# A relu behind a copy, the first queries in two transfers, and form jobs spread anew, in a three-layer kernel on one core

## The chip, the core and the metric

The kernel runs on one core of a Trainium2 chip. The metric is the device time of one execution in microseconds (us), as the median of several runs. The core has a matrix engine (TensorE, here PE, with its weight loads shown apart as PEld), a vector engine (VectorE, DVE), an activation engine (ScalarE, ACT), GpSimd (POOL) and SyncE (SP). Each works through a queue of its own in order, and semaphores tie the queues together. Transfers are issued on the queues of SP, ACT and POOL and carried out by 16 DMA engines. PE accumulates in PSUM banks; DVE and ACT read these and write to on-chip memory (SBUF). The clock that TensorE is granted has two levels here, 1.2 and 2.4 GHz, shown as 0.50 and 1.00.

## The reference

Three layers follow one another, for 4 batches of 448 positions and 768 channels (12 heads of 64):

```python
scores = q @ k.T / sqrt(64) - log(448)        # 48 heads, 448 x 448
x = sigmoid(scores) @ v                       # back to (4, 448, 768)

h = x.T @ U @ V                               # rank 32, along the positions
u = x + h.T
x = u + relu(u @ w_ch1) @ w_ch2               # 768 -> 3072 -> 768

gate = sigmoid(causal convolution of x, 5 taps a channel)
out = (gate * (x @ w_val)) @ w_out            # 768 -> 768 -> 768
```

q, k and v are float32, the weights come as float64. The products are made from a rounded part and a remainder of each factor: high by high, high by low and low by high, three matmuls in place of one (`mm3`, lines 439 to 441).

## The kernel before

**Attention** (to about 155 us) runs over 24 pairs of heads. A pair has one tile `kq`: keys of both heads on 128 partitions in `kq[:, 0]`, queries in `kq[:, 1]`. `load_kq` (L450) issues its transfers, `load_v` (L465) those of the values: 2 and 3 per pair. `kq` has three buffers. For the first two pairs the queries come in one transfer from an access pattern whose outermost step is the head (2 heads, 64 rows, 448 columns); keys and queries of the first pair go out on SP and ACT, of the second on ACT and SP. Later pairs use two SP transfers of 64 rows.

`prep_pair` (L484) makes the rounded parts `ks[:, 0]` (casts) and the remainders `ks[:, 1]` (subtractions on DVE, `low`). For the first pair the keys are cast by DVE (L494), the queries by ACT (L505). `scores` (L519) makes three 128 by 448 score tiles a pair, each from three products for each of two heads; ACT turns each into a sigmoid (L514), from one of three PSUM score tiles (`ps_s`). `scores_rest` and `attend` follow. Before the first scores PE runs `IDLE` matmuls on zeros (L1045). SP's order at the start is: first pair's keys, second pair's queries, six transfers of values, the third pair's load, constants (L654 to L662), then the fourth pair's load.

**The middle layer** (to about 834 us) has two halves, for batches 0, 1 and 2, 3, of six stages each. A stage has two chains and four `ch2` products. A chain (`seven`, L799) forms a 2 by 2 block product with seven products instead of eight. Their order is A11, A12, S2, S1, S3, S4, A22, each nine matmuls, into three PSUM banks x, y, z: A11 goes to x and is copied to p1; A12 goes to y; S2 adds to x, which is copied to u2 (L810); S1 goes to z, copied to p5; S3 adds to x, S4 adds to z, A22 adds to x. `both` (L866) adds two of them on DVE (L867) and puts off a `relu`, an ACT instruction (L861) and a DVE one (L862) that make the two parts of a hidden tile. The first of these, p1 plus y, is the chain's first sum, and its relu the chain's first relu.

Order is made while the program is written out. Steps that would wait are put in a list `deferred`, and each `flush()` writes out what is in it; `later` puts a step off by one flush more. A flush stands before each product, in some jobs, and in `weight` for as long as a weight form is not yet written.

Weights become forms by jobs (`pair_jobs`, `second_jobs`, `form_jobs`), one list for the whole layer, made by `plan`. `step()`, called after each product, takes one job off, now and then two, if the forms then held stay within `WS` = 10 tiles. `form_jobs` makes the seven or eight forms of each value and output weight block, 63 jobs in all, and stores them to memory. They are dealt out among the six stages of the second half: `share` = 13 to each until none is left, so 13, 13, 13, 13, 11, 0. In the same stages lie the gate's jobs, and at the ends of the first three the sums (`u_sums`, DVE at L600) for the value product.

**The last layer** (`val_chain`, `fin_chain`) uses `seven` too, with other `both` functions that put off no relu.

Of the kernel before, what the change touches and what calls it, by code (L numbers as in the profile page):

```python
# [12 lines left out]
AF = mybir.ActivationFunctionType  # L13
# [3 lines left out]
P = 128  # L17
B, H, S, D = 4, 12, 448, 64
# [6 lines left out]
NQ = NF // QUAD  # L25
TAPS = 5
PAD = TAPS - 1
SC = 112
# [10 lines left out]
NKC = 3  # L39
FILL = P - SC  # L40
USED = NKC * FILL
IDLE = 8
EARLY = 3
LATE = 5
PARTS = ("A11", "A12", "S2", "S1", "S3", "S4", "A22")
# [3 lines left out]
def tile_kernel(  # L49
# [18 lines left out]
    nc = tc.nc  # L68
    mm = nc.tensor.matmul
    f32 = lambda ap: ap.bitcast(F32)  # L70
    deferred = []

    def later(part):
        deferred.append(lambda: deferred.append(part))
# [99 lines left out]
    def done_with():  # L174
        live[0] -= len(spent)
        spent.clear()
# [236 lines left out]
    def ready_jobs(p):  # L413

        def job(n, half):
            def run():
                t = wtile(f"w2_{p}_{n}_{half}")
                nc.sync.dma_start(f32(t), stash["w2", n, half][:, :, :])
                forms[p, n, half] = t
            return 1, run, None  # L420

        return [job(n, half) for half in range(2) for n in range(QUAD)]
# [27 lines left out]
    def load_kq(p):  # L450

        kq = pools["kq"].tile([P, 2, S], F32, tag="kq", name=f"kq{p}")
        if p < 2:
            heads = bass.AP(
                tensor=kq_in.tensor, offset=kq_in[p, 0, 1].offset, ap=[[S, 2], [3 * S, D], [1, S]]
            )
            one, other = (nc.sync, nc.scalar) if p == 0 else (nc.scalar, nc.sync)
            one.dma_start(kq[:, 0], kq_in[p, :, 0])
            other.dma_start(kq[:, 1], heads)
        else:  # L460
            nc.sync.dma_start(kq[:D], kq_in[p, :D, :2])
            nc.sync.dma_start(kq[D:], kq_in[p, D:, 0::2])
        return kq
# [20 lines left out]
    def prep_pair(p):  # L484
        if p >= NP:
            return
        kq, vr = raws[p]
        ks = pools["ks"].tile([P, 2, 2, NSC, P], F32R, tag="ks", name=f"ks{p}")
        pairs[p] = ks, vr, {}
        rows = kq[:, :, :].rearrange("p t (c s) -> p t c s", c=NSC)  # L490
        fill = kq[:, 0, NKC * SC:NKC * SC + USED].rearrange("p (i s) -> p i s", i=NKC)

        def cast(op, r):
            op(ks[:, 0, r, :, :SC], rows[:, r])  # L494

        def low(r):
            nc.vector.tensor_sub(ks[:, 1, r, :, :SC], rows[:, r], f32(ks[:, 0, r, :, :SC]))  # L497

        if p == 0:
            cast(nc.vector.tensor_copy, 0)  # L500
        else:
            cast(nc.vector.tensor_copy, slice(0, 2))
        nc.vector.tensor_copy(ks[:, 0, 0, :NKC, SC:], fill)
        if p == 0:
            cast(lambda out, x: nc.scalar.activation(out, x, AF.Copy), 1)  # L505
            low(1)
            low(0)
        else:
            low(slice(0, 2))
        nc.vector.tensor_sub(ks[:, 1, 0, :NKC, SC:], fill, f32(ks[:, 0, 0, :NKC, SC:]))  # L510
# [288 lines left out]
    def seven(tag, weight_of, ts, both, last_of, step, before=None):  # L799

        def part(ps, ws, name, start=False):
            done_with()
            flush()
            w = weight_of(ws)
            for k in range(KH):
                mm3(ps, w, k, us[(ts, name), k], start and k == 0, k == KH - 1, skip_group_check=True)

        def copy(name, ps):
            t = pools["t"].tile([P, S], F32, tag="t", name=f"{name}_{tag}")[:, :]
            nc.scalar.activation(t, ps, AF.Copy)  # L810
            return t

        x = trio(f"x_{tag}")[:, 0, :S]
        z = bank(f"z_{tag}")[:, :S]
        part(x, "A11", "B11", True)
        p1 = copy("p1", x)
        step()
        if before:
            before()
        y = bank(f"y_{tag}")[:, :S]  # L820
        part(y, "A12", "B21", True)
        deferred.append(lambda: both(0, 0, p1, y))
        step()
        part(x, "S2", "T2")
        u2 = copy("u2", x)
        step()
        part(z, "S1", "T1", True)
        p5 = copy("p5", z)
        step()
        part(x, "S3", "T3")  # L830
        both(1, 1, p5, x)
        step()
        part(z, "S4", "B22")
        deferred.append(lambda: both(0, 1, u2, z))
        step()

        def last():
            part(x, "A22", "T4")
            last_of(x)
            step()  # L840

        return last

    def chain(p, c, step, before=None):

        b = halves[p]

        def weight_of(ws):
            w = weight(p, c, ws)
            if (p, c, ws) not in early:  # L850
                spent.append(1)
            return w

        def new(i, j):
            t = operand(f"h{c + i}_{b[j]}")
            hs[p, c + i, b[j]] = t
            return t

        def relu(i, j, x):
            t = new(i, j)  # L860
            nc.scalar.activation(t[:, 0], x, AF.Relu)  # L861
            deferred.append(lambda: nc.vector.scalar_tensor_tensor(  # L862
                t[:, 1], x, 0.0, f32(t[:, 0]), op0=ALU.max, op1=ALU.subtract
            ))

        def both(i, j, x, other):  # L866
            nc.vector.tensor_add(x, x, other)  # L867
            later(lambda: relu(i, j, x))

        return seven(f"{p}_{c}", weight_of, p, both, lambda x: relu(1, 0, x), step, before)  # L870

    def val_chain(k, gate, step, before=None):

        b = halves[0]
        z = lambda i, j: (x_of(b[j], k + KH * i), gate[k + KH * i][:, j])

        def both(i, j, x, other):
            nc.vector.tensor_add(x, x, other)
            out, g = z(i, j)
            deferred.append(lambda: nc.vector.tensor_mul(out, x, g))  # L880

        def last_of(x):
            out, g = z(1, 0)
            nc.vector.tensor_mul(out, x, g)

        return seven(f"val_{k}", lambda ws: fetched["val", k, ws, 0], "y", both, last_of, step, before)

    def fin_chain(p, k, src, step, before=None, end=False):

        b = halves[p]  # L890
        o = [pools["late"].tile([P, 2, S], F32, tag="late", name=f"o{p}_{k + KH * i}") for i in range(2)]
        have = set()

        def send(i, j):
            m = k + KH * i
            have.add((i, j))
            if end:
                nc.sync.dma_start(out[m, :, b[j]], o[i][:, j])
            elif (i, 1 - j) in have:
                nc.sync.dma_start(out[m, :, b[0]:b[-1] + 1], o[i])  # L900

        def both(i, j, x, other):
            nc.vector.tensor_add(o[i][:, j], x, other)
            send(i, j)

        def last_of(x):
            if not end:
                nc.scalar.activation(o[1][:, 0], x, AF.Copy)
                send(1, 0)
                return  # L910
            left, right = slice(0, S // 2), slice(S // 2, S)
            nc.scalar.activation(o[1][:, 0, left], x[:, left], AF.Copy)
            nc.vector.tensor_copy(o[1][:, 0, right], x[:, right])
            nc.scalar.dma_start(out[k + KH, :, b[0], left], o[1][:, 0, left])
            nc.sync.dma_start(out[k + KH, :, b[0], right], o[1][:, 0, right])

        return seven(
            f"fin{p}_{k}", lambda ws: fetched["out", k, ws, src], f"z{p}", both, last_of, step, before
        )

# [110 lines left out]
    def attention_phase():  # L1031
# [11 lines left out]
        idle = pools["ps_s"].tile([P, 2, 512], F32, tag="sc", name="idle")  # L1043
        for _ in range(IDLE):
            mm(idle[:, 0, :S], zeros[:, 0, :P], zeros[:, 0], start=True, stop=True)  # L1045
# [80 lines left out]
    def plan():  # L1126
# [9 lines left out]
        rest = []  # L1136
        for q in range(NQ):
# [17 lines left out]
            rest = w1[2:]  # L1155
# [3 lines left out]
            loads.remove(key)  # L1159
            loads.insert(len(ahead) - EARLY + 2 * i, key)  # L1160
        more = [job for kind in ("val", "out") for k in range(KH) for job in form_jobs(kind, k)]
        share = -(-len(more) // (NQ - 1))
        for q in range(NQ):
            give(pair_jobs(1, QUAD * q))
            a = pair_jobs(1, QUAD * q + 2) + (second_jobs(1, q) if q else ready_jobs(1))
            rest = more[:share]
            for i, job in enumerate(gate_jobs(halves[0], q)):
                rest.insert((2 * i + 1) * len(more[:share]) // 6 + i, (*job, None))
            for i, job in enumerate(a):
                give([job] + (rest[i // 2:i // 2 + 1] if i % 2 else []))  # L1170
            give(rest[len(a) // 2:])
            del more[:share]
# [288 lines left out]
```

## Time and profile before

| | |
|---|---|
| median of 3 runs | 1002.25 us (1001.76 to 1003.13) |
| profiled execution, whole | 1001.45 us |
| its span, first to last instruction | 999.7 us |
| PE busy | 983.3 us (98%) |
| PE weight loads | 837.9 us (84%) |
| DVE busy | 734.2 us (73%) |
| ACT busy | 463.7 us (46%) |
| mean granted TensorE clock | 0.996 |

All times within the execution count from the span's start. An engine's busy share is a mean over stages with different limits, so a shorter execution can only come from a stage where PE stands still or runs at the lower clock, or from work that PE itself no longer does. Matmuls follow each other before the one ahead has ended: a row of one matmul shows some 0.36 us, and one starts every 0.2 us.

### The profile page before, as it was taken

The numbers are of one execution on the slowest core, as the hardware profiler recorded it, in microseconds if no ns is written. First come the engines' busy times: TensorE is split into PE (matmuls) and PEld (weight loads), VectorE is DVE, ScalarE is ACT, GpSimd is POOL, SyncE is SP. The second block draws the span as 40 slices with busy tenths as digits, with TensorE's granted clock in tenths as the row PEclk, the third lists the DMA queues.
The fourth block names the chain that finished last, engine by engine and source line by source line (L and its number), as shares of the span: only waits on it lengthen the run. The fifth ranks groups of instructions, "written<-read, shape, count | busy, mean of one in ns | idle before, by whom it ended". The sixth has DMA issues, their size and how long they took to land.

```text
span 999.7 us, 14554 instructions
## 1 busy us (share of the span) xinstructions
PE 983.3 (98%) x5207; PEld 837.9 (84%) x5207; DVE 734.2 (73%) x1324; ACT 463.7 (46%) x871; POOL 22.6 (2%) x41
## 2 busy tenths in 40 slices
PE   6999999999999999999999999999999999999998
PEld 4455447988888999999999998998999999999997
DVE  2768798557668787879657988798878857993621
ACT  4657686345255363627243544536353532432321
POOL 0111200000000000000000000000000000000000
PEclk8999999999999999999999999999999999999999
DMA  5977856535447575766747555455644386834844
GB/s 139 262 201 206 216 154 172 169 87 140 138 122 220 182 220 176 219 194 206 272 145 260 186 204 195 156 201 203 220 139 176 103 311 213 277 111 128 260 152 171
DMA packets 82908, 187.51 MB, mean 188 GB/s; under 512 B 14948, under 2 KB 34644, under 8 KB 82836
## 3 DMA queue, kind: packets, MB, share of 16 engines
q1 hardware_dynamic: 78578, 171.07, 54.6%
q0 software_dynamic: 2976, 12.19, 4.1%
q10 hardware_dynamic: 1282, 3.33, 0.9%
q8 instruction: 41, 0.67, 0.3%
q14 instruction: 31, 0.25, 0.1%
HBM read 129.14 MB, written 57.41 MB: 187 GB/s over the span
## 4 chain that ended last, share of the span: by engine, by line
PE 80%; DVE 5%; ACT 1%; issue 1%; DVEq 0%; ACTq 0%
PE ch L439 12%; PE ch L440 11%; PE ch L441 11%; PE x L439 6%; PE x L441 6%; PE x L440 6%; PE z L439 3%; PE z L440 3%; PE z L441 3%; PE x_fin L439 1%; PE x_fin L441 1%; PE val L439 1%; PE val L440 1%; PE x_fin L440 1%; PE val L441 1%; PE y L441 1%
## 5 line engine op out<-in xcount | busy, mean ns | idle before, releaser
L439 PE MATMUL ch<-h,w 128*128 128x448 f32 x576 | 211.3, 367 | 0.0
L440 PE MATMUL ch<-h,w 128*128 128x448 f32 x576 | 210.5, 365 | 0.0
L441 PE MATMUL ch<-h,w 128*128 128x448 f32 x576 | 210.5, 365 | 0.0
L942 DVE TENSOR_TENSOR xs<-ch,xs 128x1344 f32<-128x1344 f32 x48 | 74.7, 1555 | 62.2 <-PE ch L441 62.1
L439 PEld LDWEIGHTS ch<-h,w 128*128 128x128 f32 x576 | 108.2, 188 | 10.5 <-issue 1.2
L441 PEld LDWEIGHTS ch<-h,w 128*128 128x128 f32 x576 | 108.2, 188 | 8.7
L440 PEld LDWEIGHTS ch<-h,w 128*128 128x128 f32 x576 | 108.2, 188 | 8.6
L514 ACT ACTIVATE a<-sc,bias 128x896 f32<-128x896 f32 x72 | 67.5, 1008 | 6.1 <-PE sc L526 5.6
L105 DVE SCALAR_TENSOR_TENSOR x_w<-x_w,r_w 128x384 uint32<-128x384 uint32 x84 | 47.0, 559 | 25.8 <-ACT x_w L101 19.4
L526 PEld LDWEIGHTS sc<-ks 64*128 64x128 f32 x432 | 38.8, 190 | 28.3 <-ACT ks L505 7.1
L526 PE MATMUL sc<-ks 64*128 64x448 f32 x432 | 53.8, 387 | 7.1 <-ACT ks L505 6.5
L557 PE MATMUL av<-a,vr 128*64 128x448 f32 x288 | 59.4, 548 | 0.1
L439 PE MATMUL x<-T,S 128*128 128x448 f32 x144 | 52.9, 367 | 2.3 <-ACT u L810 2.3
L101 ACT ACTIVATE x_w<-raw_w 128x384 f32<-128x384 f32 x84 | 45.4, 546 | 17.1 <-DMA k_h<-x_w 11.0
L441 PE MATMUL x<-T,S 128*128 128x448 f32 x144 | 52.8, 366 | 0.0
L440 PE MATMUL x<-T,S 128*128 128x448 f32 x144 | 52.6, 365 | 0.0
L557 PEld LDWEIGHTS av<-a,vr 128*64 128x64 f32 x288 | 18.5, 136 | 30.2 <-issue 26.7
L201 ACT ACTIVATE S<-raw_x_w 128x384 fp32r<-128x384 f32 x48 | 23.3, 518 | 41.7 <-DVE raw_x_w L253 21.9
L201 ACT ACTIVATE A<-x_w 128x384 fp32r<-128x384 f32 x36 | 18.3, 520 | 48.5 <-PE ch L441 43.2
L861 ACT ACTIVATE h<-p 128x448 fp32r<-128x448 f32 x48 | 27.5, 572 | 19.7 <-DVE p L867 19.7
L497 DVE TENSOR_TENSOR ks<-kq,ks 128x896 fp32r<-128x896 f32 (+1 forms) x25 | 26.3, 1055 | 7.4 <-ACT ks L505 7.4
L439 PEld LDWEIGHTS x<-T,S 128*128 128x128 f32 x144 | 27.0, 188 | 5.3 <-ACT u L810 3.0
(303 smaller groups left out, 2154.7 us busy)
## 6 DMA issues: line engine op xcount, KB each, us to landing
raw_w<-in_w SPq DMA_DIRECT2D x78, 384.0 KB, 3.7
kq<-in_kq SPq DMA_DIRECT2D x46, 224.0 KB, 4.5
raw_x_w<-k_w SPq DMA_DIRECT2D x24, 384.0 KB, 3.5
k_w<-x_w SPq DMA_DIRECT2D x42, 192.0 KB, 3.8
f_val_A<-s_val_A SPq DMA_DIRECT2D x21, 384.0 KB, 3.8
f_out_S<-s_out_S SPq DMA_DIRECT2D x20, 384.0 KB, 3.7
raw_w<-in_w POOLq DMA_DIRECT2D x18, 384.0 KB, 5.2
k_h<-x_w SPq DMA_DIRECT2D x36, 192.0 KB, 3.6
```

The source lines that it names most:

```text
L101: nc.scalar.activation(f32(x), f32(high), AF.Prelu, scale=2.0 ** -112, alpha=-(2.0 ** 32))
L105: nc.vector.scalar_tensor_tensor(x, x, 3, r, op0=ALU.logical_shift_left, op1=ALU.bitwise_or)
L201: nc.scalar.activation(t[:, 0], x, AF.Copy)
L439: mm(ps, wk[:, 0], x[:, 0], start=start, stop=False, **kw)
L440: mm(ps, wk[:, 0], x[:, 1], start=False, stop=False, **kw)
L441: mm(ps, wk[:, 1], x[:, 0], start=False, stop=stop, **kw)
L497: nc.vector.tensor_sub(ks[:, 1, r, :, :SC], rows[:, r], f32(ks[:, 0, r, :, :SC]))
L514: nc.scalar.activation(a[:, :, :], ps[:, :, :S], AF.Sigmoid, bias=bias, scale=1.0 / math.sqrt(D))
L526: mm(ps[:, h, :S].rearrange("p (c s) -> p c s", c=NSC), ks[r, tk, 0, c], ks[r, tq, 1, :, :SC], start=t == 0, stop=t == 2,)
L557: mm(att["ps"][D * h:D * h + D, :S], vr[:, h, c], a[:, h], start=c == 0, stop=False,)
L861: nc.scalar.activation(t[:, 0], x, AF.Relu)
L942: nc.vector.tensor_add(y, three[:, :, :S], y)
```

## The change

Four edits. The first pair's queries come in two transfers, one for each head, on ACT and on SP behind the keys; the second pair's load takes the form of the later ones, all on SP. The cast of these queries is split, half the partitions on ACT and half on DVE, and there are 10 idle matmuls in place of 8. In a chain the first sum is still written out at the same flush, but its relu is put into the list only once the copy of the third product has been written, and so stands behind this copy on ACT. The value and output form jobs are dealt 10, 10, 11, 14, 14 and the last 4 to the six stages, and the places of the gate's jobs among them follow the new share.

```diff
-IDLE = 8
+IDLE = 10
@@ load_kq
-        if p < 2:
-            heads = bass.AP(
-                tensor=kq_in.tensor, offset=kq_in[p, 0, 1].offset, ap=[[S, 2], [3 * S, D], [1, S]]
-            )
-            one, other = (nc.sync, nc.scalar) if p == 0 else (nc.scalar, nc.sync)
-            one.dma_start(kq[:, 0], kq_in[p, :, 0])
-            other.dma_start(kq[:, 1], heads)
+        if p == 0:
+            nc.sync.dma_start(kq[:, 0], kq_in[p, :, 0])
+            for h, queue in enumerate((nc.scalar, nc.sync)):
+                r = slice(D * h, D * h + D)
+                queue.dma_start(kq[r, 1], kq_in[p, r, 1 + h])
         else:
             nc.sync.dma_start(kq[:D], kq_in[p, :D, :2])
             nc.sync.dma_start(kq[D:], kq_in[p, D:, 0::2])
@@ prep_pair
-        def cast(op, r):
-            op(ks[:, 0, r, :, :SC], rows[:, r])
+        def cast(op, r, h=slice(0, P)):
+            op(ks[h, 0, r, :, :SC], rows[h, r])
...
         if p == 0:
-            cast(lambda out, x: nc.scalar.activation(out, x, AF.Copy), 1)
+            cast(lambda out, x: nc.scalar.activation(out, x, AF.Copy), 1, slice(0, D))
+            cast(nc.vector.tensor_copy, 1, slice(D, P))
             low(1)
             low(0)
@@ seven
         y = bank(f"y_{tag}")[:, :S]
         part(y, "A12", "B21", True)
-        deferred.append(lambda: both(0, 0, p1, y))
+        held = []
+        deferred.append(lambda: held.append(both(0, 0, p1, y, True)))
         step()
         part(x, "S2", "T2")
         u2 = copy("u2", x)
+        deferred.append(lambda: held[0] and held[0]())
         step()
@@ chain
-        def both(i, j, x, other):
+        def both(i, j, x, other, hold=False):
             nc.vector.tensor_add(x, x, other)
+            if hold:
+                return lambda: relu(i, j, x)
             later(lambda: relu(i, j, x))
@@ plan
-        share = -(-len(more) // (NQ - 1))
         for q in range(NQ):
...
+            share = (10, 10, 11, 14, 14, 10)[q]
             rest = more[:share]
             for i, job in enumerate(gate_jobs(halves[0], q)):
-                rest.insert((2 * i + 1) * len(more[:share]) // 6 + i, (*job, None))
+                rest.insert((2 * i + 1) * share // 6 + i, (*job, None))
```

## Rows read from the trace of the kernel before

**Rows 1.** Busy time by stretch: stretch, length, then PE, PEld, DVE, ACT, POOL busy, clock, DMA, GB/s.

```profile
950.00:1000.00 50.00, 45.98 (x223) 41.43 (x221) 10.98 (x19) 10.78 (x22) 0.00 (x0) 0.98 0.48 161
```

**Rows 2.** Waits of PE, whole span: waiter, releaser, us in total, times, longest.

```profile
PE x L439 <- ACT u L810: 2.3, 2, 2.0
```

**Rows 3.** Instructions in order, 0 to 28 us: start, busy, engine, line, work, [idle before].

```profile
1.42 3.35 PE L1045 MATMUL idle<-zeros 128*128 128x448 f32 x8 [1.42 <-DVE zeros L1042]
...
3.33 0.39 DVE L494 CAST ks<-kq 128x448 fp32r<-128x448 f32 x1 [1.96 <-DMA kq<-in_kq]
...
10.64 0.58 ACT L505 ACTIVATE ks<-kq 128x448 fp32r<-128x448 f32 x1 [6.85 <-DMA kq<-in_kq]
...
11.27 4.05 PE L526 MATMUL sc<-ks 64*128 64x448 f32 x18 [6.49 <-ACT ks L505]
...
12.32 0.20 DVE L510 TENSOR_TENSOR ks<-kq,ks 128x48 fp32r<-128x48 f32 x1
...
13.36 3.03 ACT L514 ACTIVATE a<-sc,bias 128x896 f32<-128x896 f32 x3 [2.15 <-PE sc L526]
...
20.60 2.11 PE L526 MATMUL sc<-ks 64*128 64x448 f32 x18
...
24.18 0.63 DVE L494 CAST ks<-kq 128x896 fp32r<-128x896 f32 x1 [2.52 <-DMA kq<-in_kq]
...
26.70 1.47 PE L526 MATMUL sc<-ks 64*128 64x448 f32 x12
```

**Rows 4.** Busy time by stretch, two single microseconds of the start; columns as in rows 1.

```profile
10.00:11.00 1.00, 0.00 (x0) 0.00 (x0) 0.00 (x0) 0.36 (x1) 0.00 (x0) 0.50 0.13 50
...
15.00:16.00 1.00, 1.00 (x12) 0.21 (x8) 0.69 (x2) 1.00 (x2) 0.00 (x0) 1.00 0.80 219
```

**Rows 5.** Transfers issued on the queues of ACT and SP, 0 to 12 us.

```profile
0.74 1.13 ACTq L459 DMA_DIRECT2D kq<-in_kq  x1
0.74 0.39 SPq L458 DMA_DIRECT2D kq<-in_kq  x1
...
2.66 2.59 SPq L472 DMA_DIRECT2D vr<-in_va  x1
...
5.93 1.54 SPq L471 DMA_DIRECT2D vr<-in_va  x1
...
11.28 0.60 SPq L476 DMA_DIRECT2D vl<-in_va  x1
```

**Rows 6.** Waits of SP's queue, 0 to 30 us.

```profile
SPq L472 <- DMA kq<-in_kq: 3.1, 1, 3.1
SPq L462 <- DMA kq<-in_kq: 1.2, 1, 1.2
```

**Rows 7.** Busy time by stage, second half: stages two, three, four and six; columns as before.

```profile
557.70:612.40 54.70, 54.70 (x272) 50.62 (x271) 48.19 (x85) 27.57 (x58) 0.00 (x0) 1.00 0.60 208
612.40:667.80 55.40, 55.17 (x272) 50.50 (x271) 46.59 (x82) 25.48 (x52) 0.00 (x0) 1.00 0.57 191
667.80:724.90 57.10, 55.08 (x272) 50.71 (x271) 49.94 (x88) 29.33 (x61) 0.00 (x0) 1.00 0.61 209
...
779.60:834.30 54.70, 54.70 (x272) 50.59 (x271) 39.02 (x56) 21.33 (x41) 0.00 (x0) 1.00 0.54 194
```

**Rows 8.** Instructions of PE, DVE and ACT in order, 673 to 678 us, fourth stage.

```profile
673.25 0.36 PE L439 MATMUL z<-T,S 128*128 128x448 f32 x1
...
675.55 0.61 DVE L867 TENSOR_TENSOR p<-p,y 128x448 f32<-128x448 f32 x1
...
676.20 0.58 ACT L861 ACTIVATE h<-p 128x448 fp32r<-128x448 f32 x1 [3.43 <-DVE p L867]
...
677.26 0.48 PE L439 MATMUL x<-T,S 128*128 128x448 f32 x1 [2.02 <-ACT u L810]
```

**Rows 9.** Transfers of the page: tiles, queue, times, KB each, median us to landing.

```profile
kq<-in_kq SPq DMA_DIRECT2D x46, 224.0 KB, 4.5
```

**Rows 10.** DVE's joins of output weights: count, ns least, median and most.

```profile
L105 DVE SCALAR_TENSOR_TENSOR x_out<-x_out,r_out x12: 558/559/561, 651.2 to 759.3; 128x384 uint32<-128x384 uint32 x12
```

More of the change, by code (lines that the diff above doesn't have):

```diff
@@ L875, in val_chain, with both @@
         z = lambda i, j: (x_of(b[j], k + KH * i), gate[k + KH * i][:, j])
-        def both(i, j, x, other):
+        def both(i, j, x, other, hold=False):
             nc.vector.tensor_add(x, x, other)
@@ L900, in send, with both @@
                 nc.sync.dma_start(out[m, :, b[0]:b[-1] + 1], o[i])
-        def both(i, j, x, other):
+        def both(i, j, x, other, hold=False):
             nc.vector.tensor_add(o[i][:, j], x, other)
```

## The prediction

> **What bounds the kernel now.** I read the page first, then a table of stages, then the waits of the matrix engine (PE), and then the two places that these name. PE is busy 98% of the span, so what can be gained is its idle time and the time it spends at the lower clock. Of the table of stages one row stands for the end [rows 1]: the last 50 us lose 4.0, of which 0.3 lie behind the span's end and the rest is the last result's way out, which nothing here touches. Most of what is left lies in the first 12 us. Behind the start, the list of waits [rows 2] has only one large entry, a copy inside a chain: two waits, 2.3 us. Every other one in it stays near 1 us or below.
>
> The start [rows 3]: eight idle matmuls end at 4.77. The keys of the first pair are there by 3.33, when DVE casts them. The queries come 7.3 us later: ACT's cast begins at 10.64, the first scores at 11.27, and PE has waited 6.49 us. Why so late is in the table by microsecond [rows 4]: at 10 us the transfers keep 0.13 of 16 DMA engines busy, that is two, at 50 GB/s. The queries' pattern has two heads as its outermost step, and ACT issues it in 1.13 us, against 0.39 us for the keys on SP [rows 5]. SP is caught too: issues of 2.59 and 1.54 us, where 0.6 is usual [rows 5], and waits of 3.1 and 1.2 us for the same transfers [rows 6]. And as PE has stood still since 4.77, its granted clock is 0.50 (1.2 GHz) at 10 us and 1.00 (2.4 GHz) again only at 15 [rows 4]; so the first 18 score matmuls take 4.05 us, where 18 later ones take 2.11 [rows 3].
>
> The chains: a stage of the second half is 270 matmuls by the code, and an undisturbed one takes 54.70 us, 0.2026 us a matmul [rows 7]. Two stages are longer, by 0.7 and 2.4 us. The larger loss is spelled out in [rows 8]: the chain's first sum stands in a full DVE queue until 675.55, ACT's relu waits for it until 676.20, the copy of the third product stands behind the relu on ACT, and PE's fifth product, which adds to the bank being copied, starts at 677.26, 2.02 us late by its row. Its due time was 675.07: 1.82 us, nine matmuls, behind the fourth product's start at 673.25. So with the pipeline's overlap 2.2 us are lost in this chain.
>
> **The change, part by part.**
> *Queries of the first pair in two transfers of 64 rows, one on ACT, one on SP.* The keys' issue stays where it is. ACT's half is issued at 0.74, SP's half behind the keys at about 1.2. The keys were in use 2.6 us after their issue; the transfers of later pairs take 4.5 us in the median [rows 9]. So ACT's half lands between 3.3 and 5.2, SP's between 3.8 and 5.7. I take 3.6 and 4.3, near the lower ends, because these are the first transfers on an empty DMA.
> *The cast in two halves.* I take each half at the duration of the whole, an upper bound: ACT's 0.58 us ends by 4.2, DVE's 0.39 us runs from 4.3 to 4.7. Behind it DVE needs what it needed before, 1.30 us from the end of the last cast (11.22) to the end of the small subtraction (12.52) [rows 3]. So all low parts are ready at 6.0 in place of 12.52. The first sigmoid followed 0.84 us behind that at 1.2 GHz; the doubled clock saves some 0.35 us of it. It starts near 6.5 and no longer at 13.36, 6.8 us earlier.
> *From there on.* The sigmoids of 1.0 us set when score banks come free, before as after; so the second pair's scores end 6.8 us earlier too, and the third pair's, at 20.60 before, start near 13.8.
> *Two more idle matmuls.* Eight took 3.35 us; ten take at most 4.2 and end by 5.6. Scores cannot pass their second step before about 5.3 nor their third before 6.0, so this is hidden. If the queries landed at 3.8, it would cost up to 0.4 us.
> *The second pair's load moves to SP, as two transfers.* SP loses its stalls: 2.0 and 0.9 us of slow issues, 3.1 and 1.2 us of waits, 7.2 in all. It gains the first pair's half (0.4) and two issues of 0.6 us in place of one of 0.70: about 1.0. So SP comes at least 6.2 us earlier to the fourth pair's load. That pair's cast began at 24.18 and its scores at 26.70 [rows 3], with a cast of 0.63 and 1.3 us of subtractions between: 0.6 us of slack, and PE's 6.8 is just covered. The second pair's load, issued by 2.9, lands by 7.4 if it takes the median of [rows 9], and is cast and split by 9.3; PE wants it near 8.9, by steps. So I take 0.1 us off.
> For the start I take **6.7 us**. Ends: 7.3 (all lands early, the slack used up) and 5.3 (SP's half at 5.7).
>
> The Trainium skill speaks against one half of this part: its page "DMA: Bandwidth & Descriptors", section "Issuing engines are not separate DMA queues", says that issuing from several engines only saves issue time; if the two queues were all, the start would gain about the 0.4 us of one issue (rival 3). The same page, section "Why a DMA increments its semaphore by 16 and not by 1", has a copy spread over the largest number of engines up to 16 that divides the slowest dimension of both sides: two for the old pattern, 16 for 64 rows. The trace agrees with the two, by its share of 0.13; the 16 are for the run after to show.
>
> *The first relu behind the third product's copy.* In the chain of [rows 8] the copy then runs as soon as its product is done, near 673.3, and the fifth product starts in time, at 675.07. The relu still waits for the sum (676.16) and ends at 676.78. Next late is the copy of the fourth product, now behind the relu: it ends near 677.25, and PE's sixth product, due at 676.89, waits 0.4 us. Of 2.2 us 1.8 are saved. The value and output chains get a call that does nothing.
> *The forms spread anew.* 63 form jobs were dealt 13, 13, 13, 13, 11, 0 over the six stages of the second half; now 10, 10, 11, 14, 14, 4. Each costs DVE about 1 us: an output form of ten jobs has four joins, four sums and seven low parts of some 0.56 us [rows 10] and four smaller steps. The stages that lose time are the third and, at its very start, the fourth; fewer form jobs before that point thin out the queue in front of the late sum. I credit 0.4 us. The later stages have the room: the fourth has 49.94 us of DVE work and gets about 1 more, the sixth 39.02 and gets 4, of 54.7; the second carried 48.19 without a loss [rows 7].
> For the chains together I take **2.2 us** of the 3.1 lost. Ends: 3.1, and -1.0 if another chain loses what the smaller of the two did and this one is not mended.
>
> **Sum.** 6.7 + 2.2 = 8.9 us. The profiled execution took 1001.45 us around a span of 999.7, and would come to 992.55 around 990.8; the median of the runs shown stands 0.8 us above it, so 1002.25 - 8.9 = **993.35 us**.
>
> **Rivals.**
> 1. *The chain's wait only moves*, to the fourth product's copy or, by the new order of forms, to another chain: 6.7 + 0.3 gives 995.25 us. For it: the sum is late because of DVE, and that stays. Against: from the second product's end PE was held if sum, relu and copy took over 3.65 us (two products), now over 5.5 (three).
> 2. *The start is caught by what comes next.* Two pairs' loads now stand on one queue, and the clock need not be up. Scores at 1.2 GHz cost 1.94 us more [rows 3], a second pair that lands 1 us late another 1: 3.8 + 2.2 gives 996.25 us. For it: the second pair's estimate above is tight. Against: PE no longer stands still for 6.5 us. The skill's page "TensorE: Matmul & The Clock Gate", section "Part 1: The HAM clock gate (the "warmup" mystery)", lets the moment of the rise vary from run to run; one trace cannot show that.
> 3. *The change does not do what it says.* If the lateness belonged to the first use of ACT's queue and not to the shape, one half would still come late: 0.4 + 2.2 gives 999.65 us. Against it: SP's own issues stalled at the same time, and two engines' share.
> 4. *Slower.* Form jobs and weight jobs draw on the same ten tiles. Dealt late, the forms hold tiles that the weights of stages four to six need; each of their six chains waits as the one in [rows 8] did, 2.2 us, and no chain gain is left: 1002.25 - 6.7 + 13.2 = 1008.75 us. It decides once a stage's DVE work passes 54.7 us; the fourth would have about 51.
>
> **How the numbers follow.** Forecast 0.61, rival 1 0.18, rival 2 0.13, rival 3 0.05, rival 4 0.03. The forecast's own ends: 7.3 + 3.1 gives 991.85, 5.3 + 1.8 gives 995.15. The range takes in rivals 1 and 2 with a quarter of a microsecond below and half of one above: 991.6 to 996.8. A measurement tells about 0.2% (2 us) from no change. Faster by more than that hold the forecast, rivals 1 and 2 and, as it lies at the edge, half of rival 3: 0.94; within 0.2%: 0.03; slower: 0.03.
>
> **What would show it.** Right: scores from about 5.5 with the granted clock at 1.00 throughout, PE's wait before them below 1 us, the first sigmoid near 6.5, the third pair's scores near 13.8, SP without a long issue; in the second half stages of 54.7 us with at most 0.5 lost in one. Wrong: a query half that lands behind 5.7, a new wait of PE for the second or third pair's cast, a wait of PE for a chain's fourth copy, or for a weight form in the last three stages.

## The result, and the profile after

| | before | after |
|---|---|---|
| median | 1002.0 us (4 runs, 999.26 to 1003.13) | 989.08 us (4 runs, 989.0 to 989.2) |
| profiled execution, whole | 1001.45 us | 989.1 us |
| its span | 999.7 us | 987.3 us |
| PE busy | 983.3 us | 979.2 us |
| mean granted clock | 0.996 | 1.000 |

The ratio is 0.9875 (95% interval 0.9855 to 0.9895): 12.9 us less, where 8.9 were forecast, and the time lies 2.5 us below the range. To see where, each matmul's start in the one trace is set against the same matmul's start in the other; what the distance between them grows by is the gain of that stretch. It is 6.5 us when the third pair's sigmoids meet their values (28.78 before, 22.31 after), loses 0.6 near 230 us of after, grows by 3.0 in stages three and four of the second half, and these three make 8.9. The rest grows in two stretches without a wait that went away: 1.1 between 156 and 215 us of before, and 2.3 from 875 us to the end.

The start after, in order (start, busy, engine, line, work, idle before), answers to [rows 3] and [rows 5]:

```profile
0.74 0.55 ACTq L457 DMA_DIRECT2D kq<-in_kq  x1
1.19 0.57 SPq L457 DMA_DIRECT2D kq<-in_kq  x1
1.42 4.10 PE L1048 MATMUL idle<-zeros 128*128 128x448 f32 x10 [1.42 <-DVE zeros L1045]
...
3.92 0.58 ACT L503 ACTIVATE ks<-kq 64x448 fp32r<-64x448 f32 x1 [1.10 <-DMA kq<-in_kq]
4.39 0.39 DVE L492 CAST ks<-kq 64x448 fp32r<-64x448 f32 x1 [0.39 <-DMA kq<-in_kq]
...
5.45 2.45 PE L525 MATMUL sc<-ks 64*128 64x448 f32 x18
...
6.72 2.81 ACT L513 ACTIVATE a<-sc,bias 128x896 f32<-128x896 f32 x3 [2.23 <-PE sc L525]
...
13.70 2.11 PE L525 MATMUL sc<-ks 64*128 64x448 f32 x18
...
18.68 0.63 DVE L492 CAST ks<-kq 128x896 fp32r<-128x896 f32 x1 [3.52 <-DMA kq<-in_kq]
...
20.49 1.89 PE L525 MATMUL sc<-ks 64*128 64x448 f32 x16 [0.21 <-DVE ks L495]
```

Both halves of the queries are cast by 4.8, the first scores follow the idle matmuls without a gap, and of PE's waits for keys or queries 0.21 us is left, for the fourth pair's remainder. SP's longest wait for such a transfer is 0.3 us, where it was 3.1 [rows 6]. The stage windows of after (columns as in [rows 1]; the first is of the start and answers to [rows 4], the others to stages three, four and six in [rows 7]; then the last layer):

```profile
5.00:6.00 1.00, 1.00 (x6) 0.30 (x4) 1.00 (x3) 0.00 (x0) 0.00 (x0) 1.00 0.98 229
...
605.40:660.10 54.70, 54.70 (x271) 50.69 (x271) 47.80 (x83) 26.62 (x55) 0.00 (x0) 1.00 0.56 193
660.10:714.90 54.80, 54.80 (x273) 50.77 (x272) 45.88 (x79) 25.78 (x54) 0.00 (x0) 1.00 0.57 202
769.60:824.30 54.70, 54.70 (x271) 50.70 (x270) 43.37 (x66) 25.40 (x50) 0.00 (x0) 1.00 0.67 241
...
870.00:970.00 100.00, 100.00 (x496) 92.66 (x495) 50.87 (x89) 26.44 (x52) 0.00 (x0) 1.00 0.55 180
```

The two stages that were 55.40 and 57.10 long are 54.7 and 54.8, and PE's waits for a copy [rows 2] are gone. The last line is the surprise when the same stretch of before is read, where PE is as busy and its clock as high:

```profile
877.00:977.00 100.00, 100.00 (x485) 90.85 (x484) 52.58 (x92) 28.50 (x57) 0.00 (x0) 1.00 0.53 170
```

The same 100 us hold 496 matmuls in the one and 485 in the other (those cut by the window's edges count too). From start to start that is 0.2027 us in after, 0.2067 in before: 2%, at a granted clock of 1.00 in both. I call them the **short** and the **long** spacing. Before's trace goes from the short to the long one at a single place (PE in order):

```profile
874.61 0.37 PE L441 MATMUL val<-y,f_val_A 128*128 128x448 f32 x1
874.83 0.47 PE L439 MATMUL x_val<-T_y,f_val_A 128*128 128x448 f32 x1
875.14 0.36 PE L440 MATMUL x_val<-T_y,f_val_A 128*128 128x448 f32 x1
```

A hitch of 0.1 us (0.47 for one matmul, 0.31 to the next), and all behind it run at the long spacing. After has the same hitch at 864.89, and keeps the short one. The 1.1 us between 156 and 215 are of the same kind: before runs that stretch at 0.2067, after at 0.2027.

### The profile page after: what moved, and what is told of

Read it like the earlier page. It is cut to its first block, busy times and chain, and to the rows that moved or that the text cites. A ratio compares the mean times of both kernels' runs of the same rounds, so it can differ in the third digit from the quotient of the medians.

```text
span 987.3 us, 14561 instructions
## 1 busy us (share of the span) xinstructions
PE 979.2 (99%) x5209; PEld 837.7 (85%) x5209; DVE 736.0 (75%) x1325; ACT 464.1 (47%) x871; POOL 22.2 (2%) x41
## 4 chain that ended last, share of the span: by engine, by line
PE 82%; DVE 3%; ACT 1%; DMA 1%; issue 0%; DVEq 0%; ACTq 0%
PE ch L439 12%; PE ch L440 12%; PE ch L441 12%; PE x L439 6%; PE x L441 6%; PE x L440 6%; PE z L440 3%; PE z L441 3%; PE z L439 3%; PE y L441 1%; PE x_fin L439 1%; PE val L439 1%; PE x_fin L441 1%; PE val L440 1%; PE y L439 1%; PE x_fin L440 1%
## 5 line engine op out<-in xcount | busy, mean ns | idle before, releaser
L863 DVE SCALAR_TENSOR_TENSOR h<-p,h 128x448 fp32r<-128x448 f32 x48 | 29.8, 620 | 6.5 <-ACT h L862 6.4
L102 DVE TENSOR_SCALAR r_w<-raw_w 128x384 uint32<-128x384 uint32 x84 | 29.8, 355 | 0.8 <-DMA raw_w<-in_w 0.5
```

What stands on the lines that cost most here:

```text
L102: nc.vector.tensor_scalar(r, low, 2.0 ** -29, 7.0, op0=ALU.mult, op1=ALU.min)
L863: deferred.append(lambda: nc.vector.scalar_tensor_tensor(t[:, 1], x, 0.0, f32(t[:, 0]), op0=ALU.max, op1=ALU.subtract))
```

## The experiments

**Each part alone, and before again.** Of the diff above, e1_start takes the three edits of the start, e2_relu those of `seven` and the `both` functions, e3_forms those of `plan`; e4_before is before, unchanged. Their key lines:

```diff
 e1_start
-            other.dma_start(kq[:, 1], heads)
+            for h, queue in enumerate((nc.scalar, nc.sync)):
...
 e2_relu
+        deferred.append(lambda: held[0] and held[0]())
 e3_forms
+            share = (10, 10, 11, 14, 14, 10)[q]
```

> Only the start of the change (first pair's queries as two transfers of 64 rows on two queues, second pair's load on SP, split cast, ten idle matmuls). Theory: the start is worth 6.9 us by the trace of after (first scores at 5.45, fourth pair's scores at 19.81 where they were at 26.70), the two late chains stay as they were: their stages stay 0.7 and 2.4 us long. Third term, the last layer: one matmul starts every 0.2067 us in before and every 0.2027 in after from about 875 us on, worth some 2.3 us. If that is a draw that any run makes when PE resumes after a short wait, this kernel may show either: 995.1 us at 0.2067, 992.8 at 0.2027. If the old order of the forms brings the slower spacing with it (rival), it shows 0.2067 here: 995.1 us.

> Only the relu behind the third product's copy. Theory of the prediction: the fourth stage loses 0.4 us in place of 2.2, the third stage keeps its 0.7 us; 1.8 us less than before at the same spacing in the last layer: 1000.2 us at 0.2067, 997.9 at 0.2027. Rival: the chain's wait moves to the copy of the fourth product and nothing is gained: 1002.0 or 999.7 us.

> Only the forms spread anew. Theory of the prediction: fewer form jobs ahead of the sums thin out the queue in front of the late sum, 0.4 us less; with the relu ahead of the copy the fourth stage still loses over 1.5 us. Rival: the new spread alone takes the late sums away, both stages come to 54.7 us: 3.1 us less. At 0.2067 us a matmul in the last layer 1001.6 against 998.9 us; at 0.2027 2.3 us less in either case. If the last layer's spacing is 0.2027 in all runs with the new spread and 0.2067 in all with the old, it belongs to the spread.

> The kernel before, unchanged, for a second trace. Theory: the spacing of matmuls in the last layer is drawn anew in each execution, so its times lie in two groups some 2.3 us apart, near 999.5 and near 1002, and this trace shows the spacing that goes with its time. Rival: it is a property of this program, 0.2067 us in this trace too, at 1002 us, and the lone time of 999.26 has another cause.

Measured, with medians of 7 to 10 runs beside 1003.07 for before (28 runs, 999.49 to 1008.43): the start alone 994.43 (ratio 0.9918, 0.9886 to 0.9949), the relu alone 1001.64 (0.9985, 0.9961 to 1.0009), the forms alone 998.42 (0.9964, 0.9931 to 0.9998), before again 1002.4 (0.9988). The three gains add up to 14.7 us, but runs of one kernel lie 7 to 13 apart, and the traces say in part why. First the relu alone, ACT in the fourth stage:

```profile
674.31 0.54 ACT L810 ACTIVATE u<-x 128x448 f32<-128x448 f32 x1 [0.67 <-PE x L441]
677.06 0.58 ACT L863 ACTIVATE h<-p 128x448 fp32r<-128x448 f32 x1 [2.21 <-DVE p L869]
677.54 0.53 ACT L810 ACTIVATE p<-z 128x448 f32<-128x448 f32 x1
```

It does what was worked out: the copy u runs when its product is done, the relu still waits 2.21 us for the late sum, and the next copy, p, is now late: PE waits 0.2 us for it. The matmuls gain 2.3 us at this place and give back 0.9 within the next six us: 1.4 in all. In the first half the same edit costs 0.6 us. The forms alone mend both chains: the trace has no wait of PE for a copy, and gains 0.7 and 2.3 us in the two (its long spacing set apart), as much as after does. They would have done it without the relu. Yet that trace took 1004.92 us, as it has the long spacing from 370 to 866 us, where 10 us go (2% of 496 us); no wait stands at either end.

What the start alone shows is the price of the wait that it keeps (PE in order, and then one microsecond of it by window):

```profile
668.30 0.37 PE L441 MATMUL z<-T,S 128*128 128x448 f32 x1
670.95 0.74 PE L439 MATMUL x<-T,S 128*128 128x448 f32 x1 [2.28 <-ACT u L809]
671.49 0.58 PE L440 MATMUL x<-T,S 128*128 128x448 f32 x1
671.86 0.58 PE L441 MATMUL x<-T,S 128*128 128x448 f32 x1
```

```profile
672.00:673.00 1.00, 1.00 (x5) 0.88 (x4) 1.00 (x3) 1.00 (x4) 0.00 (x0) 0.50 0.26 100
```

PE stood still for 2.28 us, and its granted clock is 0.50 (1.2 GHz) until 674.1: matmuls come every 0.37 us, which costs another 1.5 us. Behind that it has the long spacing until 858, 3.6 us more. Before again loses the clock behind the same wait, its window at 679.00 shows 0.50:

```profile
679.00:680.00 1.00, 1.00 (x4) 0.92 (x3) 1.00 (x3) 0.99 (x3) 0.00 (x0) 0.50 0.11 44
...
877.00:977.00 100.00, 100.00 (x494) 92.69 (x494) 54.16 (x95) 30.49 (x61) 0.00 (x0) 1.00 0.52 169
```

but its last layer, in the second line, has the short spacing, where before's first trace had the long one. So which spacing a stretch has is not fixed by the program.

**Two parts without the third.** The same edits, with one left out: e5_relu_forms has the old start, e6_no_relu the old relu, e7_no_forms the old shares.

> The relu and the forms without the start. Theory: both late chains are gone, all six stages of the second half take 54.7 us at the quick spacing; 3.1 us less than the span of before, at the same spacing: 996.3 us whole if quick from 215 us to the end (the kernel before: 999.4 at that). Rival: the two edits get in each other's way and a stage still loses over 0.5 us.

> The kernel after without the relu's move (start and forms). Theory, from the run with the forms alone, where PE waited for no copy in any chain: the forms alone mend both stages, no wait of PE for the copy u: 989.1 us if the spacing is quick throughout. Rival: with everything 6.9 us earlier the late sum comes back, and the fourth stage loses over 1 us: 990.5 us or more.

> The kernel after without the new spread (start and relu). Theory, from the run with the relu alone: two waits of 0.2 us for u and for the second p stay, stages three and four lose some 0.7 and 0.5 us together 1.2: 990.3 us if the spacing is quick throughout. Rival: both stages at 54.7, 989.1 us.

One run each: 998.57, 988.45 and 993.8 us. Without the start the stages are 54.7 us long as in after; what is missing is the start's gain and the short spacing from 872 us on. Without the forms PE waits 0.3 us for the copy u, 0.2 for the copy p and 0.2 for a sum, and has the long spacing from 674.8 to 855. Without the relu it waits for none of them, and the trace ends 0.6 us ahead of after's. That is the place near 230 us. After, ACT and then PE:

```profile
228.35 0.55 ACT L809 ACTIVATE u<-x 128x448 f32<-128x448 f32 x1 [1.36 <-PE x L441]
228.79 0.57 ACT L862 ACTIVATE h<-p 128x448 fp32r<-128x448 f32 x1
229.26 0.93 ACT L201 ACTIVATE S<-x_w 128x384 fp32r<-128x384 f32 x2
...
230.23 0.47 PE L439 MATMUL x<-T,S 128*128 128x448 f32 x1 [0.16 <-ACT S L201]
```

and without the relu's move:

```profile
228.79 0.93 ACT L201 ACTIVATE S<-x_w 128x384 fp32r<-128x384 f32 x2
229.62 0.57 ACT L860 ACTIVATE h<-p 128x448 fp32r<-128x448 f32 x1
...
229.91 0.37 PE L439 MATMUL x<-T,S 128*128 128x448 f32 x1
```

Here the sum is early and the relu, moved behind the copy, now stands ahead of the weight form S that the next product loads; the form comes 0.47 us later, and PE with it, at two matmuls.

**The start, taken apart.** After with 8 idle matmuls; with both halves on ACT; with the old two-head transfer for the first pair; and before with its two-head transfers cut into two, each on the queue it had:

```diff
 e8_idle8 (from after)
-IDLE = 10
+IDLE = 8
 e9_one_queue (from after)
-            for h, queue in enumerate((nc.scalar, nc.sync)):
+            for h, queue in enumerate((nc.scalar, nc.scalar)):
 e10_old_pattern (from after)
-            for h, queue in enumerate((nc.scalar, nc.sync)):
-                r = slice(D * h, D * h + D)
-                queue.dma_start(kq[r, 1], kq_in[p, r, 1 + h])
+            nc.scalar.dma_start(kq[:, 1], heads)
 e11_shape (from before)
-            other.dma_start(kq[:, 1], heads)
+            for h in range(2):
+                r = slice(D * h, D * h + D)
+                other.dma_start(kq[r, 1], kq_in[p, r, 1 + h])
```

> The kernel after with eight idle matmuls again. Theory: the two more hide nothing and cost nothing, as the scores wait for the casts until 5.4 us anyway: first scores at 5.4, clock 1.00 from there on, third pair's scores at 13.7. Rival: the clock needs them; it is 0.50 for the first scores, the first sigmoid comes near 7.4 in place of 6.72, and the third pair's scores 0.5 us or more later.

> The kernel after with both query halves on ACT's queue. Theory: the shape does it, not the two queues; the second half is issued at 1.3 in place of 1.19, and SP is free 0.6 us earlier: first scores between 5.3 and 5.7, third pair's scores within 0.3 us of 13.70. Rival: ACT's queue is slow at its first use: first scores behind 7.

> The kernel after with the first pair's queries in the old transfer again, two heads outermost, on ACT; all else as after. Theory: it runs on two engines, now alone on them, at some 50 GB/s for 224 KB, 4.6 us from about 2.6: it lands near 7.4, first scores near 8, the start loses 2.3 to 3.5 us against after and the DMA share is not 0.13, since the others use all engines. Rival: the second pair's transfer on the same two engines was the whole lateness, and first scores come before 6.5.

> The kernel before with one thing changed: each two-head query transfer of the first two pairs is cut into two of 64 rows on the queue where it was. Theory: nearly all of the start's 6.9 us comes from this: ACT's second half is issued at 1.3 and lands near 4.4, ACT casts until 5.0, first scores near 5.1, third pair's scores near 13.9. Rival: the split cast and SP's load of the second pair count too: third pair's scores behind 14.7, 1 us or more short of after.

One run each: 989.05, 992.54, 998.53 and 1001.37 us. *Eight idle matmuls* cost nothing: scores begin at 4.70, but wait for remainders, and the third pair's come at 13.94; from 22.31 on the two traces agree. *One queue* was expected to change nothing (third pair's scores within 0.3 us of after's). ACT, DVE and PE in order:

```profile
4.43 0.58 ACT L503 ACTIVATE ks<-kq 64x448 fp32r<-64x448 f32 x1 [0.96 <-DMA kq<-in_kq]
5.45 0.74 PE L525 MATMUL sc<-ks 64*128 64x448 f32 x1
6.25 0.39 DVE L492 CAST ks<-kq 64x448 fp32r<-64x448 f32 x1 [1.89 <-DMA kq<-in_kq]
6.70 4.35 PE L525 MATMUL sc<-ks 64*128 64x448 f32 x17 [0.51 <-DVE ks L492]
...
17.53 2.10 PE L525 MATMUL sc<-ks 64*128 64x448 f32 x18
```

The second half is cast 1.9 us later than in after. Then 17 scores take 4.35 us, the rate that before had at 0.50 in [rows 3, 4]. The windows' clock column shows 1.00 here, but it does so at 2 us in every trace, where idle matmuls start every 0.37 us, and at 10 us in e4_before, where PE stands still and before has 0.50. Up to a trace's first change of clock the column tells nothing, so I go by the matmuls. That holds for the 1.00 of after's window at 5 us as well; its scores start every 0.20 us from 6.7 on. The third pair's scores come 3.8 us behind after's, and 3.4 are left in the end. The Trainium skill's page "DMA: Bandwidth & Descriptors", section "Issuing engines are not separate DMA queues", has a second issuing engine save no more than issue time. Worked out from the rows, that is 0.6 us for one issue. 3.4 were measured, but this run does not test that sentence by itself, as the order of the loads changed too: with the half off SP, the second pair's load goes out at 1.19 and no longer at 1.80, beside the late half and not behind it. That fits the lateness; that it is the cause is not shown. By the matmuls 1.2 us are lost at the second score, and the rest behind it, at the lower rate.

*The old pattern* for this one transfer, with its engines' share at 10 us:

```profile
11.33 0.39 DVE L493 CAST ks<-kq 64x448 fp32r<-64x448 f32 x1 [7.24 <-DMA kq<-in_kq]
11.96 4.30 PE L526 MATMUL sc<-ks 64*128 64x448 f32 x18 [6.75 <-ACT ks L504]
```

```profile
10.00:11.00 1.00, 0.00 (x0) 0.00 (x0) 0.00 (x0) 0.00 (x0) 0.00 (x0) 0.50 0.14 43
```

It alone brings the whole loss back, and more: the third pair's scores come at 22.52, 8.8 us behind after's, where I had expected some 3 us. At 10 us it still runs, on 0.14 of 16 engines at 43 GB/s. SP's queue stands as well: it issues nothing between 5.06 and 11.32. *The shape alone*, in before:

```profile
6.22 0.58 ACT L504 ACTIVATE ks<-kq 128x448 fp32r<-128x448 f32 x1 [2.03 <-DMA kq<-in_kq]
6.85 4.29 PE L525 MATMUL sc<-ks 64*128 64x448 f32 x18 [2.07 <-ACT ks L504]
```

The queries come 4.4 us earlier by the shape, but PE has stood still for 2.07 us and its scores take 4.29 us again. Only 3.2 us are left by the third pair (17.42 against 20.60 before, 13.9 expected). The shape is what made the transfer late; how much of that is gained depends on the rest of the start (order of the loads, split cast, clock), which these runs do not tell apart. This trace, too, keeps the chain's wait, has the clock at 0.50 behind it, and the long spacing until 862; it also has it from 567 to 617.

**After again, and without the relu.** e12_after and e15_after are after, unchanged. e13_no_relu is e6_no_relu once more. e14_lean is that kernel with one step of the last layer's gate work put off, which in the traces lies in front of the hitch in the value chain:

```diff
-                run(budget)
+                if at[0] != 18:
+                    run(budget)
```

> The kernel after, unchanged, on the chip of these runs. Theory: PE's spacing of matmuls, 0.2027 or 0.2067 us, is drawn where PE resumes after a wait, and can change; after keeps three of the waits at which the kernel before redraws it out of the long layer, so its times lie closer together, near 989.1, and seldom above 992. Rival: the spacing is drawn by the chip or the hour alone, and its times here spread over some 9 us as those of before did (999.5 to 1008.4), from 989 to 998.

> The kernel after without the relu's move, timed in rounds beside after itself. Theory: the forms alone mend the two late chains, and the relu's move only puts the relu ahead of weight casts that PE is about to need (0.6 us lost at 230 us in the trace of after): 0.6 us less than after at the same spacing, 988.4 us when quick throughout. Rival: the two are equal within 0.2 us, or after is faster.

> Without the relu's move, and one DVE step of the gates (three instructions of some 1.2 us) put off by one product in the last value chain, so that the sum in front of PE's last wait, at 864 us, is 2.3 us earlier. Theory: PE then has no wait above 0.15 us from 160 us to the end, nothing redraws its spacing, and the last layer goes on at the spacing of the middle layer: 0.2 us less than without the edit when quick, and no time 2 us above the lowest one from this cause. Rival: the spacing in the last layer changes in its runs too, with no wait in front of it.

> The kernel after, unchanged, beside the run without the relu's move. Theory: 989.1 us when its spacing is quick from 150 us on, up to 992 when the last layer draws the slow one; the lowest time lies 0.6 us above the lowest of the run without the relu's move. Rival: no difference between the lowest times.

After gave 991.97 us on one chip (3 runs, 990.02 to 992.96, not near the 989.1 expected; before 1006.14) and 989.91 on another (4 runs; ratio 0.9859, 0.9815 to 0.9902; before 1004.2). On the latter e13 gave 991.99 (4 runs, 990.89 to 992.58) and e14 989.44 (4 runs, 989.29 to 989.84; ratio 0.9856). The traces tell them apart by the last layer. After at 992.96 us:

```profile
870.00:970.00 100.00, 100.00 (x485) 90.84 (x484) 51.14 (x90) 27.62 (x55) 0.00 (x0) 1.00 0.54 173
```

485 where after's first trace has 496; e13's trace has 486, those of e14 and e15 have 496. So leaving the relu alone is worth 0.6 us between two traces of equal spacing, and no median shows it: the draw is worth 2. In e14's trace the hitch is gone. But its runs lie within those of e15 (988.99 to 990.34), so it is not shown to be better than after.

**Does a wait draw the spacing anew?** In the output chains the third product goes ahead of the second, so that it meets the copy p1 too early and PE waits (the main lines):

```diff
+        if late:
+            part(x, "S2", "T2")
+            u2 = copy("u2", x)
+            step()
```

> Without the relu's move; in the six output chains the third product stands ahead of the second, so that PE waits for ACT's copy of the first product, some 0.7 us each: about 4 us longer, 992.5 us if all is quick. Theory: the spacing is drawn where PE resumes, so it may change at these six places (near 905, 918, 931, 944, 957 and 970 us) and at no other place between them. Rival: the last layer keeps one spacing through all six waits.

991.46 us, and only the first of six chains waited; in the others the last product of the chain ahead lies between. I had expected 4 us of waits. But that one tells something (PE in order, then a window ahead of it and one behind):

```profile
910.03 0.37 PE L441 MATMUL x_fin<-B_z,f_out_A 128*128 128x448 f32 x1
911.03 0.47 PE L439 MATMUL x_fin<-T_z,f_out_S 128*128 128x448 f32 x1 [0.63 <-ACT p_fin L809]
911.34 0.36 PE L440 MATMUL x_fin<-T_z,f_out_S 128*128 128x448 f32 x1
```

```profile
868.00:908.00 40.00, 40.00 (x196) 36.33 (x195) 23.36 (x42) 8.57 (x17) 0.00 (x0) 1.00 0.38 111
914.00:974.00 60.00, 60.00 (x298) 55.61 (x297) 26.55 (x46) 18.38 (x37) 0.00 (x0) 1.00 0.71 224
```

From start to start that is 0.2067 us ahead of the wait and 0.2027 behind it: the long spacing ends exactly there.

A wait is not needed, though. e7_no_forms, two windows of equal length and the matmuls at their border:

```profile
815.00:855.00 40.00, 40.00 (x196) 36.28 (x194) 32.33 (x39) 15.03 (x23) 0.00 (x0) 1.00 0.69 230
855.00:895.00 40.00, 40.00 (x199) 36.92 (x198) 37.28 (x59) 15.67 (x28) 0.00 (x0) 1.00 0.49 155
```

```profile
855.00 0.36 PE L439 MATMUL x_val<-T_y,f_val_A 128*128 128x448 f32 x1
855.19 0.36 PE L440 MATMUL x_val<-T_y,f_val_A 128*128 128x448 f32 x1
```

The long spacing ends without wait or hitch (0.204 us to the first of these two, 0.196 to the second). e1, e3 and e11 lose it at the same matmul of the program, give or take one (858.51, 865.97, 862.62); there the other 14 traces wait 0.15 to 0.18 us for the sum p_val. Three more changes have neither wait nor hitch: e3 at 369.8 and e5 at 370.0, at the same place in opposite directions, and e11 at 567.4. Each of the seven matmuls, or the one ahead of it, has a semaphore to wait for, as one in nine has, but it was set by then. So the places recur from kernel to kernel, and PE need not be held at them.

## Why the prediction was right and wrong

**The start** was right, term by term. The halves were in use at 3.92 and 4.39 (3.6 and 4.3 taken), the first scores came at 5.45 (5.5), the first sigmoid at 6.72 (6.5), the third pair's scores at 13.70 (13.8), and the fourth pair's waited 0.21 (0.1). The sum was 6.7, and 6.5 was measured. Rival 3, ACT's first use of its queue, is out: with the old pattern the query is late on the same queue, with the new one it is not. Rival 2 did not occur, but scores at the lower rate exist, in e9 and e11, which lose 3.4 and 3.7 us where I gave it 2.9; late queries are a part of both. In after the idle matmuls run on until the queries are there; it struck where these came 1.9 us later, or where PE stood still for 2. The first 18 scores took 2.45, 2.75 and 3.07 us in three traces of after itself; the Trainium skill's page "TensorE: Matmul & The Clock Gate", section "Part 1: The HAM clock gate (the "warmup" mystery)", lets the clock's rise vary from run to run, and these three agree.

**The chains** came to 2.4 (3.0 gained, 0.6 lost), with 2.2 forecast, but for the wrong reason: that the sum fits is luck. I credited the relu with 1.8 and the forms with 0.4. Alone, the relu gains 1.4 in stage four and loses 0.6 in the first half; the forms alone gain 3.0, all that there is. After's own rows of that chain, answering to [rows 8]:

```profile
664.90 0.62 DVE L868 TENSOR_TENSOR p<-p,y 128x448 f32<-128x448 f32 x1
...
665.63 0.36 PE L439 MATMUL z<-T,S 128*128 128x448 f32 x1
...
665.83 0.55 ACT L809 ACTIVATE u<-x 128x448 f32<-128x448 f32 x1 [1.35 <-PE x L441]
...
667.10 0.57 ACT L862 ACTIVATE h<-p 128x448 fp32r<-128x448 f32 x1
```

The sum starts 0.73 us ahead of the fourth product, and in [rows 8] 2.30 behind it: 3 us earlier. By then 31 form jobs and not 39 have been dealt out; that this is how the new spread does it is argued, that the spread does it is shown by e3. With an early sum the relu could have stood on either side of the copy (e6). What I priced by one sentence ("thin out the queue") was the whole repair. And I looked for the price of the relu's move only where it helps; that the first relu moves in all 24 chains, past whatever stands next on ACT, was not asked. Rival 1's late fourth copy appears where the sum stays late (e2, e7), at 0.2 us. Rival 4 fell: the fullest of the stages shown has 47.8 us of DVE work, and the fourth 45.9 where I had 51; the work went to the fifth and sixth, which have 45.2 and 43.4 us where they had 42.6 and 39.0.

**The sum** is where it failed. That the profiled execution "would come to 992.55" takes it that every matmul outside the terms costs after what it cost before, 0.2026 us, and that the last 50 us are "the last result's way out, which nothing here touches". 3.4 us of the 12.3 between the traces lie in just that: 1.1 in the first stage and 2.3 in the last layer, at the same clock, with no wait but a hitch of 0.1 us. This also refutes what I wrote beside the profile of before, that a shorter execution can only come from idle PE, a lower clock or less work. [Rows 1] had it in plain sight: 45.98 us of PE time over 223 matmuls are 0.2062 each, where [rows 7] have, counted the same way, 54.70 over 272 or 0.2011, and I read the stretch for its idle time alone. In 18 traces the last layer has the short spacing in 11 and the long in 7 (e16, which changes within it, counted here), and before and after each have it both ways. The first stage has either in 9, and after's own traces show both. So these 3.4 us of the difference between the two traces were drawn, not made by the change.

That does not explain medians of four and more. There after gained 12.9, 14.2 and 14.3 us in three sets of runs, each time more than the 8.9 of the terms. What the traces show is that the wait that I priced at its length can cost more: of the four traces that keep it at 2 us, three have the clock at 0.50 for 3.4 us behind it (some 1.5 us), and two of these the long spacing up to 860 (3.6 us). Before's runs spread over 999 to 1011 us and after's over 989 to 993, and this would be a part of it. It is not all: the forms alone have no such wait, yet spread over 995 to 1008. The start alone keeps the wait and gains 8.6 us by its median (5.1 to 11.4 by the interval) where its term is 6.5. Between 215 and 670 us the long spacing occurs in three of the seven traces whose first scores come behind 6 us (e3, e5, e11), and in none of the eleven where they come earlier, which hints that the start has a share in it; no run tests that.

**Open** is what sets the spacing, and so where the 4 to 5 us beyond the terms come from. Nothing found in the profile foretells which spacing it will be. The range was too narrow for the same reason: its ends were bounds of the terms (the two lower ends given for the chains, -1.0 and 1.8, do not even agree), and had nothing for draws of 2 to 10 us in the kernel before, which three runs within 1.4 us did not show.

## What to carry to other kernels

Count matmuls in equal windows of a busy PE before taking a stretch as untouched: 2% over some hundred microseconds is as much as a repaired wait, and the idle columns don't show it. Price a long wait in an otherwise full stream at its length plus what the clock and the spacing behind it may cost, and get more than three runs of a kernel before taking its spread. If two parts of a change mend the same wait, price each alone, and for a step that is moved in a helper look at every call of it, not at the one that it is meant for.

## What the hardware showed that was not expected

- Two steady spacings of the same matmul at a granted clock of 1.00, 0.2027 and 0.2067 us; both in the same program, with changes at waits of 0.2 to 2.3 us, at hitches of 0.1 us, and seven times without either, four of these at one and the same place of the program.
- Behind a wait of 2.0 to 2.3 us in a full stream the clock was at 0.50 for 3.4 us in three of four traces.
- A transfer that runs on two engines was in use 10.6 us after its issue, the same queries in halves 3.2, and SP's queue issued nothing for 6.3 us meanwhile.
- Of the profile, not of the chip: ahead of a trace's first change the clock column shows 1.00, even where 17 scores run at the rate of 0.50 (4.35 us).
